# Three of the last output stores, cut into unequal runs of partitions

## The chip, the core and the metric

The kernel runs on one core of a Trainium2 chip. A core has five engines that work side by side: TensorE (matrix products, PE in the profile), VectorE (DVE), ScalarE (ACT), GpSimd (POOL) and SyncE (SP), which here issues the transfers. The transfers between the chip's large memory (HBM) and the core's working memory (SBUF, 128 partitions) are carried out by 16 DMA engines. The metric is the device time of one execution in microseconds (us), the median of several runs; lower is better.

## The reference

The computation has two stages. The first is an attention through 49 "agent" vectors per batch: the agents attend to all keys of a batch and gather a value each, and then each query attends to the 49 agents.

```
a2k = softmax(scale * agents @ k^T);  agent_v = a2k @ v        # per batch, 49 x 128
q2a = softmax(scale * q @ agents^T);  x = q2a @ agent_v        # 12,544 x 128 per batch
```

The second is a feed-forward block on all 4 x 12,544 = 50,176 rows, with a maximum over three products:

```
h = max(max(x @ w1, x @ w2), x @ w3);  out = h @ w_out         # 128 -> 768 -> 128
```

q, k, v and the output have 50,176 x 128 numbers of 4 bytes each, 25.7 MB apiece, so the kernel moves more than 100 MB through the DMA engines.

## The kernel before

The keys and values of a batch are loaded in pieces of up to four groups of seven tiles (a tile is 128 rows), cast to 16 bits, turned, scored against the agents and summed up. When a batch's 49 agent values are known, the feed-forward weights are folded into small tables for that batch (`G`), so that a query row needs only its 49 attention weights and these tables. A count made on the chip (`fullest`) decides between this short way and a general way (`in_general`); with the inputs here the short way is taken.

The queries are worked in 49 groups `s` of eight tiles (1,024 rows); 48 of them lie within a batch, and group 48 (`NQ - 1`) gathers the last two tiles of each of the four batches. Three groups share one load of q (`q_load`) and one output buffer of 128 partitions x 24 tile rows (`OS`, five of them). For each group the program casts q (POOL), turns it (PE), copies it out (ACT), scores it (PE), takes exponentials (ACT), makes the sums and two hidden products (PE), takes their maximum (ACT and DVE), makes the output product (PE) and scales it into the output buffer, in two halves of four tiles (`out_scale`; steps `ov.s.0` and `ov.s.1`).

A partition of the output buffer holds consecutive output rows, so a store is 128 pieces, one for each partition. Up to group 44, three groups are stored by one transfer (12 KB from each partition, 1,536 KB in all). Groups 45 and 46 are stored alone (step `st.45`, `st.46`: 4 KB from each partition, 512 KB), group 47 in two halves (`st.47.0`, `st.47.1`: 2 KB from each partition, 256 KB), and group 48 alone, with 1 KB pieces, 512 KB.

The order of the work is written out by hand in `ORDER`; each engine does its own steps in that order, and waits on semaphores where a step needs another engine's result. All stores and loads of this stage are issued by SyncE, one after another, from the function `store` (line 497) and its counterparts for loads (lines 288, 332, 489). At the end of `ORDER` stand

```
... st.44 x.45/1 ex.47/0 x.46/2 p.45/7,5 su.47 p.46/1,2 ov.45.0/1 u.47/0
re.47/3 v.47/4 ov.45.1 a.47/0 ov.46.0 st.45 ov.46.1 x.47/0 st.46 p.47/3,7 ov.47.1 ov.47.0 st.47.0 st.47.1
```

so group 48 is stored before group 44's buffer, and the last four transfers of the program are `st.45`, `st.46`, `st.47.0` and `st.47.1`. No later step uses their buffers again; the program's end (line 753 in the profile) waits until all stores have landed. Line 209 loads the agents, a transfer of 49 partitions issued by ScalarE at the start.

Of the kernel before, what the change touches and what calls it, by code (L numbers as in the profile page):

```python
# [16 lines left out]
P, H, C, A, B, NT, GT, KT, NF = 128, 64, 128, 49, 4, 98, 8, 7, 6  # L17
# [7 lines left out]
CAPACITY = 64  # L25
TG, TK = 3, 4
LONG = TG * GT

PE, ACT, DVE, POOL, SP = range(5)

SLOTS = {"M": 8, "LD": 5, "QB": 3, "KB": 3, "VB": 4, "KT": 3, "QT": 3, "EQ": 8, "EK": 4, "AS": 3, "R": 3, "RC": 9, "OS": 5}
SHAPE = {"LD": ([P, max(TK * KT, LONG), C], FP32), "QB": ([P, GT, C], BF16), "KB": ([P, KT, C], BF16), "VB": ([P, KT, C], BF16),
         "KT": ([P, KT * C], BF16), "QT": ([P, GT, P], BF16), "EQ": ([P, 512], BF16), "EK": ([P, KT * A], BF16),
         "AS": ([P, 512], BF16), "R": ([P, 512], BF16), "RC": ([P, GT], FP32), "OS": ([P, LONG, C], FP32)}

# [158 lines left out]
class Emit:  # L194
# [277 lines left out]
    def far(self, name, s, n):  # L472
# [6 lines left out]
        row = (z // WHOLE * NT + z % WHOLE * GT) * P  # L479
        rows = flat[row:row + LONG * P, :].rearrange("(p j) c -> p j c", j=LONG)  # L480
        return rows if n == LONG else rows[:, s % TG * GT:(s % TG + 1) * GT, :]

    def near(self, s, tile_, n):
        if s == NQ - 1:
            return tile_[:, :GT, :].rearrange("p (b j) c -> p b j c", j=2)
        return tile_[:, :LONG, :] if n == LONG else tile_[:, s % TG * GT:(s % TG + 1) * GT, :]

    def q_load(self, s):
        return lambda: self.nc.sync.dma_start(self.near(s, self.t[f"q.{s}"], LONG), self.far("q", s, LONG))

    def store(self, s, h=None):
        def fn():
            n = LONG if s < NQ - 1 - TG else GT
            far, near = self.far("out", s, n), self.near(s, self.t[f"os.{s // TG * TG}"], n)
            if h is not None:
                far, near = (x[:, self.tiles(s, h), :] for x in (far, near))
            self.nc.sync.dma_start(far, near)
        return fn

    def tiles(self, s, h, mixed=False):  # L500
# [257 lines left out]
```

## Time and profile before

| what | value |
|---|---|
| time, median of 3 runs | 257.96 us (257.70 to 258.14) |
| span of the profiled execution, first to last instruction | 256.1 us |
| busy: PE, DVE, ACT, POOL | 187.4, 163.3, 145.3, 145.7 us |
| DMA: moved in the span, mean rate | 105.00 MB, 410 GB/s |
| HBM read and written | 78.74 and 25.69 MB |

The profile has no other time of the profiled execution than its span; the runs' median is 1.9 us more, which is what lies around the first and the last instruction.

The page's second part cuts the span into 40 equal slices of 6.4 us, one digit or number for each: a digit is a busy share in tenths. Its third part counts DMA packets by queue: q1 is the queue that SyncE fills, q10 ScalarE's, and q8 and q14 bring instructions to the engines. Its sixth part, and the list of DMA issues, name each kind of transfer by where it goes and where it comes from, with how often it was issued, its size, and the median time from issue to landing. A row of a view by stages gives a stretch of the span, its length, the busy time of each computing engine with its count of instructions, the granted clock of TensorE, the mean busy share of the 16 DMA engines and their rate. A row on a line's instructions gives the shortest, the median and the longest duration in nanoseconds, and when the first and the last of them began.

### The profile page before, as it was taken

How to read it: one execution, taken by the hardware profiler on the slowest of the kernel's cores; microseconds unless marked ns; L12 is line 12 of the kernel's file. 1: busy time of each engine (PE TensorE's matmuls, PEld its weight loads, DVE VectorE, ACT ScalarE, POOL GpSimd, SP SyncE). 2: the span in 40 equal slices, each digit the busy share in tenths (PEclk: the TensorE clock that was granted, in tenths of full speed). 3: DMA queues.
4: the chain of work that ended last, by engine and by line, in shares of the span. 5: the costliest groups of instructions: out<-in, count | busy, mean ns of one | idle time of the engine just before them, and what ended most of it. 6: DMA issues, size and time to landing. Idle time of an engine off the chain costs nothing. (4 is left out here: it accounts for less than half of the span.)

```text
span 256.1 us, 7498 instructions
## 1 busy us (share of the span) xinstructions
PE 187.4 (73%) x3070; PEld 136.6 (53%) x3105; DVE 163.3 (64%) x336; ACT 145.3 (57%) x240; POOL 145.7 (57%) x164
## 2 busy tenths in 40 slices
PE   0684675869698779895986898778687779998400
PEld 0472543757475558674774677356464465664200
DVE  4443523837677868765699954724739989888700
ACT  2445357347585657573767656546256868887300
POOL 2252752998789279787975897468364443440000
PEclk9996599799999959998899999979979999999955
DMA  7999999999999999999999999999999999999993
GB/s 252 438 418 422 420 428 425 422 425 423 421 415 424 430 424 426 428 417 426 416 431 427 419 429 420 432 424 425 420 430 424 420 421 425 425 424 425 414 360 103
DMA packets 11526, 105.00 MB, mean 410 GB/s; under 512 B 1175, under 2 KB 2395, under 8 KB 4443
## 3 DMA queue, kind: packets, MB, share of 16 engines
q1 hardware_dynamic: 11280, 104.34, 97.2%
q8 instruction: 26, 0.43, 0.7%
q10 hardware_dynamic: 203, 0.10, 0.2%
q14 instruction: 17, 0.14, 0.1%
HBM read 78.74 MB, written 25.69 MB: 408 GB/s over the span
## 5 line engine op out<-in xcount | busy, mean ns | idle before, releaser
L298 POOL CAST KB<-LD 128x896 bf16<-128x896 f32 x56 | 51.8, 964 | 38.1 <-DMA LD<-in_k_dram 36.8
L508 POOL CAST QB<-LD 128x1024 bf16<-128x1024 f32 x49 | 49.8, 1048 | 33.4 <-PE psum L271 17.3
L568 DVE TENSOR_TENSOR OS<-psum,RC 128x512 f32<-128x512 f32 x97 | 60.7, 676 | 9.1 <-DMA out_dram<-OS 5.3
L514 ACT ACTIVATE QT<-psum 128x1024 bf16<-128x1024 bf16 x49 | 50.2, 1024 | 21.3 <-PE psum L303 19.6
L309 DVE COPY KT<-psum 128x896 bf16<-128x896 bf16 x56 | 34.5, 620 | 32.6 <-PE psum L303 28.6
L303 PE MATMUL psum<-ident,KB 128*128 128x128 bf16 x392 | 37.0, 246 | 11.7 <-POOL KB L298 9.9
L527 ACT ACTIVATE EQ<-psum 128x512 bf16<-128x512 f32 x49 | 29.3, 598 | 21.9 <-PE psum L271 16.0
L298 POOL CAST VB<-LD 128x896 bf16<-128x896 f32 x42 | 38.2, 949 | 4.9 <-DMA LD<-in_v_dram 4.6
L318 ACT ACTIVATE EK<-psum 128x343 bf16<-128x343 f32 x56 | 25.3, 460 | 24.7 <-PE psum L271 15.5
L303 PEld LDWEIGHTS <-KB 128*128 128x128 bf16 x392 | 28.4, 111 | 18.9 <-POOL KB L298 15.4
L547 ACT ACTIVATE AS<-psum 128x512 bf16<-128x512 f32 x49 | 29.2, 599 | 13.5 <-PE psum L271 12.4
L550 DVE TENSOR_TENSOR R<-psum,AS 128x512 bf16<-128x512 f32 x49 | 32.5, 678 | 6.4 <-PE psum L271 3.1
L303 PE MATMUL psum<-ident,QB 128*128 128x128 bf16 x392 | 31.5, 226 | 6.4 <-POOL QB L508 5.7
L303 PEld LDWEIGHTS <-QB 128*128 128x128 bf16 x392 | 25.8, 101 | 15.6 <-POOL QB L508 8.4
L271 PE MATMUL psum<-QT,agT 128*128 128x512 bf16 (+1 forms) x82 | 25.7, 380 | 6.7 <-ACT QT L514 5.9
L271 PEld LDWEIGHTS <-EQ 49*128 49x128 bf16 (+1 forms) x588 | 20.7, 97 | 16.3 <-ACT EQ L527 7.6
L271 PE MATMUL psum<-EQ,G 128*128 128x512 bf16 (+1 forms) x91 | 28.0, 367 | 1.3 <-issue 0.6
L271 PEld LDWEIGHTS <-VB 128*128 128x128 bf16 x392 | 16.6, 97 | 17.6 <-ACT VB L296 8.7
L271 PE MATMUL psum<-EK,VB 128*128 128x49 bf16 x392 | 19.7, 187 | 6.0 <-ACT VB L296 5.0
L271 PE MATMUL psum<-G,EQ 49*128 49x128 bf16 x392 | 21.4, 225 | 0.9 <-DVE OS L568 0.5
L271 PE MATMUL psum<-agT,KT 128*128 128x49 bf16 x392 | 20.5, 191 | 1.4 <-DVE KT L309 0.9
L271 PE MATMUL psum<-G,R 64*128 64x128 bf16 x392 | 20.5, 225 | 1.4 <-DVE R L550 1.4
(83 smaller groups left out, 180.7 us busy)
## 6 DMA issues: line engine op xcount, KB each, us to landing
LD<-in_q_dram SPq DMA_DIRECT2D x16, 1536.0 KB, 17.2
out_dram<-OS SPq DMA_DIRECT2D x15, 1536.0 KB, 20.0
LD<-in_k_dram SPq DMA_DIRECT2D x12, 1792.0 KB, 16.0
LD<-in_v_dram SPq DMA_DIRECT2D x12, 1792.0 KB, 16.7
LD<-in_k_dram SPq DMA_DIRECT2D x4, 896.0 KB, 16.4
LD<-in_v_dram SPq DMA_DIRECT2D x4, 896.0 KB, 14.6
out_dram<-OS SPq DMA_DIRECT2D x3, 512.0 KB, 13.0
LD<-in_moe_w_dram SPq DMA_DIRECT2D x3, 384.0 KB, 13.4
```

The source lines that it names most:

```text
L271: self.nc.tensor.matmul(out, w, x, start=start, stop=True, skip_group_check=True)
L298: self.nc.gpsimd.tensor_copy(out=out, in_=src)
L303: self.nc.tensor.transpose(t[:, j * P:(j + 1) * P], src[:, j, :], self.ident)
L309: return lambda: self.nc.vector.tensor_copy(out=self.t[f"kT{r}"], in_=self.t[f"kT_ps{r}"].bitcast(BF16)[:, :KT * C])
L318: return lambda: self.nc.scalar.activation(self.t[f"e{r}"], self.t[f"s{r}"][:, :KT * A], AF.Exp, scale=SCALE)
L508: return lambda: self.nc.gpsimd.tensor_copy(out=self.t[f"qb.{s}"], in_=self.half("q", s))
L514: return lambda: self.nc.scalar.activation(self.t[f"qT.{s}"].rearrange("p j c -> p (j c)"), self.t[f"qT_ps.{s}"].bitcast(BF16), AF.Copy)
L527: return lambda: self.nc.scalar.activation(self.t[f"e.{s}"], self.t[f"qs.{s}"], AF.Exp, scale=SCALE)
L547: return lambda: self.nc.scalar.activation(self.t[f"a.{s}"], self.t[f"u.{s}"], AF.Relu)
L550: return lambda: self.nc.vector.tensor_tensor(out=self.t[f"r.{s}"], in0=self.t[f"v.{s}"], in1=self.t[f"a.{s}"], op=ALU.max)
L568: self.nc.vector.tensor_tensor(out=out, in0=src, in1=rc.unsqueeze(2).to_broadcast([P, 4, C]), op=ALU.mult)
```

## The change

A table `PARTS` names two stores, by group and half: the store of group 45, whole, and the first half of group 47's. `store` now issues a store as a sequence of transfers over consecutive runs of partitions: 124 and 4 for group 45, 68 and 60 for the first half of group 47, and all 128 at once (`P` is 128) for every other store, as before. The same bytes go to the same places. SyncE issues two transfers more than before, 22 stores in place of 20.

```diff
 TG, TK = 3, 4
 LONG = TG * GT
+PARTS = {(45, None): (124, 4), (47, 0): (68, 60)}
...
             far, near = self.far("out", s, n), self.near(s, self.t[f"os.{s // TG * TG}"], n)
             if h is not None:
                 far, near = (x[:, self.tiles(s, h), :] for x in (far, near))
-            self.nc.sync.dma_start(far, near)
+            first = 0
+            for rows in PARTS.get((s, h), (P,)):
+                self.nc.sync.dma_start(far[first:first + rows], near[first:first + rows])
+                first += rows
         return fn
```

## The prediction

> **What bounds the kernel now.** I read the page's slices first, then SyncE's waits, then the busy time by stage at the end, then the DMA queues and issues. The page:
>
> ```profile
> span 256.1 us, 7498 instructions
> DMA  7999999999999999999999999999999999999993
> GB/s 252 438 418 422 420 428 425 422 425 423 421 415 424 430 424 426 428 417 426 416 431 427 419 429 420 432 424 425 420 430 424 420 421 425 425 424 425 414 360 103
> ```
>
> All 16 DMA engines are busy from the second slice to the last but two, at about 425 GB/s, so the kernel is bound by bytes moved. The last slices (6.4 us each) fall to 360 and 103 GB/s: the drain is not level. The waits of SyncE's queue over the last 20 us say who waits for that drain:
>
> ```profile
> SPq L753 <- DMA out_dram<-OS: 11.2, 2, 10.6
> SPq L497 <- DVE OS L568: 4.3, 3, 2.1
> ```
>
> L753 is the end of the program. SyncE stands there 10.6 us in one wait, for stores to land. The last store (the second half of group 47) has these rows among the store line's instructions:
>
> ```profile
> L497 SPq DMA_DIRECT2D out_dram<-OS x1: 615/615/615, 242.6 to 242.6; - x1
> DMA to landing us min/median/max: 11.9/11.9/11.9
> ```
>
> Issued at 242.6 and landed 11.9 us later, at 254.5 (254.6 unrounded). From there to the span's end lie 1.5 us of closing semaphores. So the end is set by the engine that empties its queue last. The stages (length; then busy time of PE, PEld, DVE, ACT, POOL; granted clock, DMA share, GB/s):
>
> ```profile
> 240.00:242.00 2.00, 0.40 (x8) 0.23 (x8) 1.51 (x3) 0.53 (x3) 0.00 (x0) 1.00 0.99 415
> 245.00:246.00 1.00, 0.00 (x0) 0.00 (x0) 0.00 (x0) 0.00 (x0) 0.00 (x0) 0.50 1.05 371
> 246.00:247.00 1.00, 0.00 (x0) 0.00 (x0) 0.00 (x0) 0.00 (x0) 0.00 (x0) 0.50 0.78 326
> 247.00:248.00 1.00, 0.00 (x0) 0.00 (x0) 0.00 (x0) 0.00 (x0) 0.00 (x0) 0.50 0.80 328
> 248.00:249.00 1.00, 0.00 (x0) 0.00 (x0) 0.00 (x0) 0.00 (x0) 0.00 (x0) 0.50 0.77 317
> 249.00:250.00 1.00, 0.00 (x0) 0.00 (x0) 0.00 (x0) 0.00 (x0) 0.00 (x0) 0.50 0.69 281
> 251.00:252.00 1.00, 0.00 (x0) 0.00 (x0) 0.00 (x0) 0.00 (x0) 0.00 (x0) 0.50 0.52 141
> 252.00:253.00 1.00, 0.00 (x0) 0.00 (x0) 0.00 (x0) 0.00 (x0) 0.00 (x0) 0.50 0.29 88
> 253.00:254.00 1.00, 0.00 (x0) 0.00 (x0) 0.00 (x0) 0.00 (x0) 0.00 (x0) 0.50 0.16 61
> 254.00:255.00 1.00, 0.00 (x0) 0.00 (x0) 0.00 (x0) 0.00 (x0) 0.00 (x0) 0.50 0.01 4
> ```
>
> Share times 16 is the number of engines still at work. From 246 to 249 it is about 12.5: some four engines are through by about 247. A fifth goes at about 249.5 (share 0.69, 11). At 251 to 252 eight work, at 252 to 253 four or five, at 253 to 254 two or three, and nothing much after 254.1. Between the first engine and the last lie some 7 us; a level drain would end earlier.
>
> How a store is spread over the engines is read from the packet counts of the whole span:
>
> ```profile
> DMA packets 11526, 105.00 MB, mean 410 GB/s; under 512 B 1175, under 2 KB 2395, under 8 KB 4443
> q1 hardware_dynamic: 11280, 104.34, 97.2%
> q8 instruction: 26, 0.43, 0.7%
> q10 hardware_dynamic: 203, 0.10, 0.2%
> q14 instruction: 17, 0.14, 0.1%
> LD<-in_q_dram SPq DMA_DIRECT2D x16, 1536.0 KB, 17.2
> out_dram<-OS SPq DMA_DIRECT2D x15, 1536.0 KB, 20.0
> LD<-in_k_dram SPq DMA_DIRECT2D x12, 1792.0 KB, 16.0
> LD<-in_v_dram SPq DMA_DIRECT2D x12, 1792.0 KB, 16.7
> LD<-in_k_dram SPq DMA_DIRECT2D x4, 896.0 KB, 16.4
> LD<-in_v_dram SPq DMA_DIRECT2D x4, 896.0 KB, 14.6
> out_dram<-OS SPq DMA_DIRECT2D x3, 512.0 KB, 13.0
> LD<-in_moe_w_dram SPq DMA_DIRECT2D x3, 384.0 KB, 13.4
> LD<-in_q_dram SPq DMA_DIRECT2D x1, 512.0 KB, 21.6
> out_dram<-OS SPq DMA_DIRECT2D x2, 256.0 KB, 11.9
> LD<-in_moe_w_out_dram SPq DMA_DIRECT2D x1, 384.0 KB, 13.7
> ag_st<-in_agents_dram ACTq DMA_DIRECT2D x1, 98.0 KB
> ```
>
> SyncE issues 73 transfers, all of 128 partitions; ScalarE one, the agents: 49 partitions of 4 rows, 196 packets. Its queue q10 shows 203, so 7 are over. And 73 x 16 + 7 = 1175, the count under 512 B. So a transfer ends with one small packet for each engine that took part: 16 engines for 128 partitions, 7 for 49. Sixteen and seven are the largest divisors of 128 and 49 not above 16; even shares of whole partitions give just that.
>
> **The change part by part.** By that rule 124 = 4 x 31 and 4 = 4 x 1 go over four engines, 68 = 4 x 17 over four, 60 = 15 x 4 over fifteen. The Trainium skill, DMA: Bandwidth & Descriptors, section "Why a DMA increments its semaphore by 16 and not by 1", states the same rule and adds that a SyncE or ScalarE transfer takes the lowest-numbered k engines; the trace's 203 agrees with the count, and no row here shows the numbers.
>
> Bytes on each of the four engines, taking the same four each time. Store of group 45 (512 KB, 4 KB a partition): 8 partitions each before, 32 after, so 24 x 4,096 = 98,304 bytes more. First half of 47 (256 KB, 2 KB a partition): 8 before, 17 + 4 after, 13 x 2,048 = 26,624 more. On each other engine: 8 x 4,096 + 4 x 2,048 = 40,960 bytes less (one engine of them 8 x 2,048 still less, as 60 goes over fifteen).
>
> Rate of one engine: 415 / (16 x 0.99) = 26.2 GB/s in 240 to 242, and 328 / (16 x 0.80) = 25.6 in 247 to 248. So the four get 98,304 / 26.2 + 26,624 / 25.6 = 3.75 + 1.04 = 4.8 us more, the others 1.6 us less. No other work hides it: after 242.6 only stores run, and the end waits for the last engine of all.
>
> The rest is small. SyncE issues two transfers more, by the store line's and the agents' rows:
>
> ```profile
> L497 SPq DMA_DIRECT2D out_dram<-OS x20: 332/346/2782, 67.7 to 242.6; - x20
> L209 ACTq DMA_DIRECT2D ag_st<-in_agents_dram x1: 577/577/577, 0.7 to 0.7; - x1
> ```
>
> An issue costs 0.35 us, 0.58 for the one that was split unevenly, 2.8 us at worst, where the queue seems to have been full. Behind the second issue of group 45 stands the store of 46, 1.2 us later (240.4 against 239.2), which covers it; behind that of 47's first half stands its second half, pushed by 0.35 to 0.6 us. It is covered by what the engines still have queued: even the first engines work until 246.5, some four us after that issue. If the queue is full for 2.8 us per issue, the last half starts at 248, still before the late engines are through. I take nothing. No compute waits: the output buffer's places are not taken again after group 45.
>
> So the time hangs on which four engines these are. An engine that ended at f ends at f + 4.8. Against the old last end, 254.1, it is harmless only for f below 249.3, and by the stages only four engines, or a fifth just about, are that early. Lower bound: the four are the early ones; they end at 247.5 + 4.8 = 252.3, the others at 254.1 - 1.6 = 252.5, which is 1.6 us gained. Upper bound: one of the four is the last engine, 4.8 us lost.
>
> Which of them is nearer? All wide transfers are shared evenly, so what makes an engine late is work beside them: instruction fetches (26 of 16 KB, 0.7% of 16 x 256.1 us, 1.1 us each, and 17 smaller ones) and the agents' load on its seven. Joining packet records end to start, I find only one of the early engines among the seven that took the agents. No view prints that, so it chooses between the cases and sets no term. If a split by four takes four of those seven, at least three late engines get the extra bytes. The latest of three out of eleven late ones ends, by the stages, between 253 and 254.1; I take 253.7. Sum: 253.7 + 4.8 - 254.1 = 4.4 us more, span 260.5. The profiled execution is told by its span alone, 256.1; the median of the runs is 257.96, 1.9 us above it for what lies around. Forecast: 257.96 + 4.4 = 262.4.
>
> **The rivals.** (1) Faster: the four engines are the early ones. Price -1.6 us, 256.4. It decides from the point where all four are through by about 249. For it: four engines are early, and the amount moved would just level the drain (252.3 against 252.5). Against it: the joined packets.
>
> (2) Nothing moves: the split is over all engines whatever the rows, or the pace is set by where a partition is read and not by the engine that reads it. Then a row moved to an idle engine still waits behind the rows of its old neighbours, the drain ends where it ended, and two issues of 0.35 us are covered: 258.0. Against the first half: 203 packets. For the second: all stages run at one rate near 425 GB/s, whatever the transfer. The Trainium skill, the same page, section "Where 436 GB/s comes from", holds that the SBUF's 16 ports of 27.2 GB/s are what limits; the 26.2 above is near it, and no row parts engine from port. By it, rival 1 would gain nearly nothing, and the forecast would come out somewhat worse, since rows read through one port by two engines go slower.
>
> (3) Slower, but less: the three others of the four are the earliest of the late ones, through by 251.4: 251.4 + 4.8 - 254.1 = 2.1 us, 260.1. (4) Slower still: the last engine is among them and shares ports at half pace for the last 1.5 us: 4.8 + 1.5 = 6.3, 264.3.
>
> **How the numbers follow.** Forecast 0.55, rival 1 0.24, rival 2 0.08, rival 3 0.09, rival 4 0.04. About 0.2% is what a measurement can tell (0.5 us). Faster 0.24, same 0.08, slower 0.68. The likeliest case alone reaches from 260.1 to 263.6 (4.8 plus 0.8 for shared ports). Leaving rival 1 out would leave more than 2 in 10 outside, so the range goes down to it: 256.2 to 263.6.
>
> **What the changed profile would show.** The count under 512 B: 1175 before; two more issues on 4 + 4 + 4 + 15 engines in place of 16 + 16 make it 1170. If it is 1207, all 16 were used. The stages: after 253 a share of about 0.2 (three or four engines) for some 5 us, with the last landing near 259 and SyncE's wait at L753 near 15 us. If the early engines took the bytes, the share stays near 1 until 251 and falls at once by 252.6. My forecast fails at its one weak step, which engines the split by four takes; the sizes before it come from counts.

## The result and the profile after

The changed kernel takes 261.14 us (median of 4 runs, 260.94 to 261.93) against 257.88 us for the kernel before on the same chip. The ratio is 1.0129, with a 95% interval of 1.0115 to 1.0144: 3.3 us slower. The forecast was 262.4, 4.4 us slower than the 257.96 it started from. Two stores are cut, those of group 45 and of the first half of group 47, though the title speaks of three.

The page of the changed kernel, in 40 slices of now 6.5 us, and its packet counts:

```profile
span 259.3 us, 7500 instructions
DMA  7999999999999999999999999999999999999961
GB/s 254 438 413 426 423 425 425 419 423 428 420 418 426 427 426 427 420 430 419 417 433 425 426 421 428 426 415 425 429 423 428 417 434 421 427 422 421 391 239 41
DMA packets 11521, 105.00 MB, mean 405 GB/s; under 512 B 1170, under 2 KB 2390, under 8 KB 4438
```

Up to the last three slices nothing has changed; there the rate is 391, 239 and 41 GB/s, against 414, 360 and 103 before. The count of small packets is the forecast 1170: the two cut stores went over 4 + 4 + 4 + 15 engines, not over 16 each.

SyncE's waits over the end, and the last store among the store line's instructions (line 500 now, which was 497):

```profile
SPq L757 <- DMA out_dram<-OS: 11.8, 4, 9.6
L500 SPq DMA_DIRECT2D out_dram<-OS x1: 1357/1357/1357, 244.6 to 244.6; - x1
DMA to landing us min/median/max: 13.3/13.3/13.3
```

The last store is issued at 244.6 (242.6 before) and lands 13.3 us later, at 257.9 (254.6 before). The forecast had SyncE's wait at the program's end near 15 us. It is 11.8 us in four pieces, the longest of 9.6, against 11.2 in two before, the longest of 10.6, because SyncE came to it 2.7 us later: the last issue began 2 us later and took 1.4 us in place of 0.6, as if the queue were full, though no view shows how full it is. So the wait does not tell the loss; the landing does, 3.3 us. The end by stages (length, then busy time of PE, PEld, DVE, ACT, POOL, granted clock, DMA share, GB/s):

```profile
249.00:250.00 1.00, 0.00 (x0) 0.00 (x0) 0.00 (x0) 0.00 (x0) 0.00 (x0) 0.50 0.81 315
250.00:251.00 1.00, 0.00 (x0) 0.00 (x0) 0.00 (x0) 0.00 (x0) 0.00 (x0) 0.50 0.48 180
251.00:252.00 1.00, 0.00 (x0) 0.00 (x0) 0.00 (x0) 0.00 (x0) 0.00 (x0) 0.50 0.39 117
252.00:253.00 1.00, 0.00 (x0) 0.00 (x0) 0.00 (x0) 0.00 (x0) 0.00 (x0) 0.50 0.22 76
253.00:254.00 1.00, 0.00 (x0) 0.00 (x0) 0.00 (x0) 0.00 (x0) 0.00 (x0) 0.50 0.26 100
254.00:255.00 1.00, 0.00 (x0) 0.00 (x0) 0.00 (x0) 0.00 (x0) 0.00 (x0) 0.50 0.15 59
255.00:256.00 1.00, 0.00 (x0) 0.00 (x0) 0.00 (x0) 0.00 (x0) 0.00 (x0) 0.50 0.13 51
256.00:257.00 1.00, 0.00 (x0) 0.00 (x0) 0.00 (x0) 0.00 (x0) 0.00 (x0) 0.50 0.06 25
257.00:258.00 1.00, 0.00 (x0) 0.00 (x0) 0.00 (x0) 0.00 (x0) 0.00 (x0) 0.50 0.04 14
```

Share times 16 again: from 252 to 254 about four engines work (0.22, 0.26), then two (0.15, 0.13), then one. The twelve others are through by about 252, some two microseconds sooner than before. The time went to a few engines that drain alone.

### The profile page after: what moved, and what is told of

It is laid out like the page before. It is cut to its first block, busy times and chain, and to the rows that moved or that the text cites. A ratio compares the mean times of both kernels' runs of the same rounds, so it can differ in the third digit from the quotient of the medians.

```text
span 259.3 us, 7500 instructions
## 1 busy us (share of the span) xinstructions
PE 188.9 (73%) x3070; PEld 138.1 (53%) x3105; DVE 163.8 (63%) x336; ACT 145.4 (56%) x240; POOL 145.7 (56%) x164
## 2 busy tenths in 40 slices
DMA packets 11521, 105.00 MB, mean 405 GB/s; under 512 B 1170, under 2 KB 2390, under 8 KB 4438
## 4 chain that ended last, share of the span: by engine, by line
DMA 49%; PE 18%; DVE 10%; POOL 8%; ACT 5%; issue 3%; SPq 0%; DVEq 0%; ACTq 0%; POOLq 0%
DMA LD<-in_v_dram 18%; DMA LD<-in_k_dram 14%; PE psum L272 13%; DMA out_dram<-OS 9%; DMA LD<-in_moe_w_dram 5%; PE psum L304 5%; POOL VB L299 4%; DVE OS L572 3%; POOL KB L299 2%; DMA ag_st<-in_agents_dram 2%; ACT VB L297 1%; ACT EQ L531 1%; ACT QT L518 1%; POOL QB L512 1%; DVE gap L407 1%
## 5 line engine op out<-in xcount | busy, mean ns | idle before, releaser
L304 PE MATMUL psum<-ident,QB 128*128 128x128 bf16 x392 | 32.4, 229 | 6.7 <-POOL QB L512 5.9
L551 ACT ACTIVATE AS<-psum 128x512 bf16<-128x512 f32 x49 | 29.2, 600 | 11.8 <-PE psum L272 10.7
L304 PEld LDWEIGHTS <-QB 128*128 128x128 bf16 x392 | 26.5, 103 | 16.3 <-POOL QB L512 8.8
L272 PE MATMUL psum<-G,EQ 49*128 49x128 bf16 x392 | 20.8, 222 | 0.7 <-DVE OS L572 0.3
## 6 DMA issues: line engine op xcount, KB each, us to landing
LD<-in_v_dram SPq DMA_DIRECT2D x4, 896.0 KB, 14.5
```

Of the source, the lines that this page charges most:

```text
L272: self.nc.tensor.matmul(out, w, x, start=start, stop=True, skip_group_check=True)
L304: self.nc.tensor.transpose(t[:, j * P:(j + 1) * P], src[:, j, :], self.ident)
L551: return lambda: self.nc.scalar.activation(self.t[f"a.{s}"], self.t[f"u.{s}"], AF.Relu)
```

## Experiments

Each experiment changes only the table `PARTS` of the changed kernel. The times before were 257.85 us for the first four runs, 257.96 for the next four and 257.79 for the last two.

**One cut alone.**

```diff
-PARTS = {(45, None): (124, 4), (47, 0): (68, 60)}
+PARTS = {(45, None): (124, 4)}
```

> Only the store of group 45 is cut, 124 and 4. In the changed kernel the last landing came at 257.9 against 254.6 before; the two cuts together put 4.8 us on each of four engines, so the latest of the four would have landed at 253.1 without them. Theory (the four lowest engines carry the extra bytes, and the time is that of the last engine): 253.1 + 3.75 = 256.9, 2.3 us more than before, 260.2. Rival (the time follows from the number of transfers or from the queue being full when they are issued): half of the whole loss, 259.5, or nothing, as the later half store is not cut.

Measured: 260.66 us, ratio 1.0119 (1.0103 to 1.0135), 2.8 us slower; last landing 257.2.

```diff
-PARTS = {(45, None): (124, 4), (47, 0): (68, 60)}
+PARTS = {(47, 0): (68, 60)}
```

> Only the first half of group 47 is cut, 68 and 60. Theory: the four engines get 1.04 us more and the others 0.3 us less, and the four are not the last ones (253.1 against 254.6 at the landing): 253.1 + 1.04 = 254.1 against 254.6 - 0.3 = 254.3, so no loss and perhaps 0.3 us gained, 257.6 to 257.9. Rival (cost by transfer, or each cut has its own price that adds up): the loss of both less that of group 45, about 1 us, 258.9.

Measured: 258.47 us, ratio 1.0023 (1.0013 to 1.0033), 0.6 us slower; last landing 255.2. Most of the loss is group 45's, as its bytes say. The loss of 0.6 us lies between the theory's none and the rival's 1 us. The two losses add up to 3.4 against the 3.3 of both together; a maximum over engines need not have added up so neatly. The trace's semaphore updates (one for each engine of a transfer, when its share has landed) put the loss on one of the four: the part of 68 partitions lands last at 254.3 and the last store 0.9 us later, just as in the changed kernel (257.0 and 257.9). These two runs leave it open whether the latest of the four engines was a little ahead of the last one, or was itself the last and a byte cost less than the rate says.

**As many transfers, evenly cut.**

```diff
-PARTS = {(45, None): (124, 4), (47, 0): (68, 60)}
+PARTS = {(45, None): (64, 64), (47, 0): (64, 64)}
```

> Both stores cut, but 64 and 64, which 16 divides: two transfers more, as in the changed kernel, and every engine's bytes as before. Theory: no change, 257.9 (within 0.5 us); packets under 512 B 1175 + 32 = 1207. Rival (cost by transfer, or SyncE held up by a full queue): as the changed kernel, 261.1.

Measured: 257.32 us, ratio 0.9982 (0.9973 to 0.9991). Packet counts, and the last store's issue and landing:

```profile
DMA packets 11558, 105.00 MB, mean 411 GB/s; under 512 B 1207, under 2 KB 2427, under 8 KB 4475
L500 SPq DMA_DIRECT2D out_dram<-OS x1: 1102/1102/1102, 244.6 to 244.6; - x1
DMA to landing us min/median/max: 9.6/9.6/9.6
```

The last store is issued at 244.6, with SyncE held up for 1.1 us, just as in the changed kernel, and it lands at 254.2, not at 257.9. So neither the two more transfers nor the later issue is what costs: with the same number of each, the time is even 0.5 us under the kernel before. The small gain was not expected.

**The lowest engine alone.**

```diff
-PARTS = {(45, None): (124, 4), (47, 0): (68, 60)}
+PARTS = {(45, None): (96, 31, 1)}
```

> Only group 45, cut 96, 31 and 1: 96 goes over sixteen engines (6 partitions each), 31 and 1 have no divisor but 1 and should go to a single engine, the lowest. That engine gets 30 partitions of 4 KB more, 122,880 bytes, 4.7 us; the fifteen others two partitions less, 0.3 us. Theory (the lowest engine is the one early engine among the four): it ends at 247.5 + 4.7 = 252.2, the last at 0.3 us less than before: 257.6, not slower. Rival (the lowest engine is as late as the others, or one engine alone cannot keep its pace): 251.5 to 254 + 4.7, 1.5 to 4.7 us more, 259.5 to 262.6.

Measured: 257.26 us, ratio 0.9975 (0.9966 to 0.9984). Packet counts, the last store's landing and the end by stages:

```profile
DMA packets 11528, 105.00 MB, mean 411 GB/s; under 512 B 1177, under 2 KB 2397, under 8 KB 4445
DMA to landing us min/median/max: 9.6/9.6/9.6
252.00:253.00 1.00, 0.00 (x0) 0.00 (x0) 0.00 (x0) 0.00 (x0) 0.00 (x0) 0.50 0.25 86
253.00:254.00 1.00, 0.00 (x0) 0.00 (x0) 0.00 (x0) 0.00 (x0) 0.00 (x0) 0.50 0.02 8
```

1175 and two more is 1177: the parts of 31 and of 1 partition each ended with one small packet, so each went over one engine. That engine bore 4.7 us more, nearly what each of the four bears in the changed kernel, and the drain ended no later: it was one of the early ones. The Trainium skill, DMA: Bandwidth & Descriptors, section "Why a DMA increments its semaphore by 16 and not by 1", has a split by one, two or four begin at the same lowest engine. The runs agree so far as the one engine that is early here is also among the four (below); the number of an engine stands in no view.

**The bytes of one more store.**

```diff
-PARTS = {(45, None): (124, 4), (47, 0): (68, 60)}
+PARTS = {(45, None): (124, 4), (46, None): (124, 4), (47, 0): (68, 60)}
```

> The changed kernel, with the store of group 46 cut 124 and 4 as well: the four engines get another 98,304 bytes each, 3.75 us by the rate of the profile. This tells two readings of the size apart. Reading A (a byte costs an engine what the profile's rate says, and the latest of the four would have ended about 1 us ahead of the last engine): the last landing moves by the full 3.75, from 257.9 to 261.7, time 261.1 + 3.75 = 264.9. Reading B (the latest of the four was the last engine of all, and the bytes moved cost 0.7 of the price, as 3.3 against 4.8, 2.8 against 3.75 and 0.6 against 1.04 suggest): 0.7 x 3.75 = 2.6, time 263.7.

Measured: 265.02 us, ratio 1.0269 (1.0255 to 1.0284). That is 3.9 us over the changed kernel, for the 3.75 of reading A and the 2.6 of reading B: A holds. The end by stages:

```profile
252.00:253.00 1.00, 0.00 (x0) 0.00 (x0) 0.00 (x0) 0.00 (x0) 0.00 (x0) 0.50 0.27 109
253.00:254.00 1.00, 0.00 (x0) 0.00 (x0) 0.00 (x0) 0.00 (x0) 0.00 (x0) 0.50 0.28 117
254.00:256.00 2.00, 0.00 (x0) 0.00 (x0) 0.00 (x0) 0.00 (x0) 0.00 (x0) 0.50 0.26 103
256.00:258.00 2.00, 0.00 (x0) 0.00 (x0) 0.00 (x0) 0.00 (x0) 0.00 (x0) 0.50 0.20 81
258.00:260.00 2.00, 0.00 (x0) 0.00 (x0) 0.00 (x0) 0.00 (x0) 0.00 (x0) 0.50 0.13 50
260.00:262.00 2.00, 0.00 (x0) 0.00 (x0) 0.00 (x0) 0.00 (x0) 0.00 (x0) 0.50 0.06 25
```

Here the four engines stand by themselves: a share of a quarter from 252 to 256, four of sixteen, and then three, two and one. Each runs at about 25 GB/s (103 / (16 x 0.26)), near the 26.2 with all sixteen at work. The trace's semaphore updates for the part of 124 partitions come at 249.1, 250.9, 253.1 and 254.9: the four are not alike, the first is 5.8 us ahead of the fourth. SyncE was held up more here: three of its issues took 2.3 to 3.4 us, and the last store was issued only at 249.4. That cost nothing, for twelve engines had landed their share of it by 252.7, and the other four did at 256.6 to 262.2.

**The two lowest engines.**

```diff
-PARTS = {(45, None): (124, 4), (47, 0): (68, 60)}
+PARTS = {(45, None): (80, 46, 2)}
```

> Only group 45, cut 80, 46 and 2: 80 goes over sixteen engines (5 each), 46 and 2 over two (23 + 1 each), so the two lowest engines get 21 partitions of 4 KB more, 3.3 us, the others 0.5 us less. The lowest engine was seen to bear 4.7 us. Theory (of the four only the lowest is early): the second ends past the old end, if it would have ended after 251.3 (254.6 - 3.3): up to 3 us more, 258.5 to 261. Rival (the two lowest are both early, and the loss comes from the third and fourth): 0.3 to 0.5 us less, 257.4.

Measured: 257.99 us, ratio 1.0004 (0.9995 to 1.0013): no change. Each of the two got 3.3 us more and neither made the end later, so the second is through early as well, if less so; the rival's gain did not come either. Together with the four landings above: two of the four have time to spare, the third and the fourth have not, and the loss comes from these. The changed kernel's own trace agrees: the part of 68 partitions lands on the four at 253.4, 253.7, 255.5 and 257.0, and the last four updates of the last store come 0.9 to 1.0 us behind these, at 254.3, 254.6, 256.4 and 257.9. Two lie no later than the old end, 254.6, and two behind it.

**Even cuts: what they do by themselves.**

```diff
-PARTS = {(45, None): (124, 4), (47, 0): (68, 60)}
+PARTS = {(45, None): (96, 32)}
```

> Only group 45, cut 96 and 32, both over sixteen engines: no byte changes its engine's total, one transfer more. The 96, 31 and 1 cut gained 0.6 us and the 64 and 64 cuts gained 0.5 us. If the gain of 96, 31 and 1 is the lowest engine's help (0.3 us by the bytes), this one gains nothing: 257.85. If a cut as such gains (a transfer more, other partitions for each engine), it gains as the others did: 257.3.

Measured: 257.59 us, ratio 0.9984 (0.9975 to 0.9993). A cut that moves no byte between engines gains 0.4 us, most of what the cut 96, 31 and 1 gained. So the run with 96, 31 and 1 shows that the lowest engine can bear 4.7 us at no cost; a gain from its help is not shown.

```diff
-PARTS = {(45, None): (124, 4), (47, 0): (68, 60)}
+PARTS = {(45, None): (96, 31, 1), (47, 0): (64, 64)}
```

> Group 45 cut 96, 31 and 1 (the lowest engine helps), the first half of 47 cut 64 and 64. If the two gains are separate things they add: 257.85 - 0.6 - 0.5 = 256.8. If both are the same thing (a later issue of the last stores, or the cut as such), 257.3 again.

Measured: 257.64 us, ratio 0.9987 (0.9975 to 0.9999). The gains do not add; if anything there is less than with either cut alone.

```diff
-PARTS = {(45, None): (124, 4), (47, 0): (68, 60)}
+PARTS = {(44, None): (64, 64), (45, None): (64, 64), (46, None): (64, 64), (47, 0): (64, 64), (47, 1): (64, 64)}
```

> The stores of groups 42 to 44, 45, 46 and both halves of 47 are cut 64 and 64: five transfers more, no engine's bytes changed. If each cut over sixteen engines gains by itself (one gained 0.4 us, two 0.5 us), five gain more, 256.9 or less. If the gain is a single small shift of when the last stores are issued, it stays at 0.3 to 0.6 us, 257.4. If a full queue holds SyncE up, the last store comes late: 258.5 or more.

Measured: 260.63 us, ratio 1.0110 (1.0091 to 1.0129), 2.8 us slower with the same bytes on every engine. The page counts 1255 small packets, 1175 and 5 x 16: every part went over sixteen engines. The store line's last issues and their landings, and then the stages:

```profile
L500 SPq DMA_DIRECT2D out_dram<-OS x2: 588/978/1367, 251.4 to 252.8; - x2
DMA to landing us min/median/max: 3.2/3.6/4.0
```

```profile
250.00:252.00 2.00, 0.00 (x0) 0.00 (x0) 0.00 (x0) 0.00 (x0) 0.00 (x0) 0.50 0.61 201
252.00:254.00 2.00, 0.00 (x0) 0.00 (x0) 0.00 (x0) 0.00 (x0) 0.00 (x0) 0.50 0.63 174
254.00:256.00 2.00, 0.00 (x0) 0.00 (x0) 0.00 (x0) 0.00 (x0) 0.00 (x0) 0.50 0.36 88
```

The last two stores are issued at 251.4 and 252.8, nine and ten microseconds after the last computing instruction, and land within 3.2 to 4.0 us: now it is the issue that is late. SyncE's issues took up to 2.8 us each, which I read as a full queue, and from 252 to 254 ten engines still work (0.63 x 16) where four or five, and then two or three, did before. So two more transfers were covered in the changed kernel, but five are not.

**The same cut far from the end.**

```diff
-PARTS = {(45, None): (124, 4), (47, 0): (68, 60)}
+PARTS = {(2, None): (124, 4)}
```

> No store of the end is cut; the first store of the run (groups 0 to 2, 12 KB from each partition, issued near 68 us) is cut 124 and 4. Each of the four engines gets 24 x 12,288 = 294,912 bytes more, 11.3 us by the rate of the profile. Theory (an engine that falls behind while all are fed evenly never catches up): the latest of the four, about 1.1 us ahead of the last engine without it, ends the run: 11.3 - 1.1 = 10.2 us more, 268.1. Rival (behind lies time enough to make up for it; only a cut at the end costs): 258 to 260.

Measured: 273.21 us, ratio 1.0601 (1.0583 to 1.0618), 15.4 us slower. The page's slices (of 6.8 us) and the longest of SyncE's waits between 80 and 115 us:

```profile
DMA  7999999999999974899999999999999999999960
GB/s 265 436 419 414 429 422 427 423 420 425 426 422 415 420 292 176 316 413 418 335 431 381 424 425 402 432 424 419 430 427 427 420 426 408 420 429 417 393 242 18
SPq L289 <- DMA LD<-in_q_dram: 17.8, 1, 17.8
```

Three stages, in the middle and at the end:

```profile
100.00:102.00 2.00, 0.00 (x0) 0.00 (x0) 0.00 (x0) 0.00 (x0) 0.00 (x0) 0.50 0.26 111
104.00:106.00 2.00, 0.83 (x7) 0.48 (x5) 0.17 (x1) 1.02 (x1) 1.80 (x3) 0.50 0.26 113
267.00:269.00 2.00, 0.00 (x0) 0.00 (x0) 0.00 (x0) 0.00 (x0) 0.00 (x0) 0.50 0.07 29
```

The cost is not made up over the 190 us that follow; it is half as large again as the forecast 10.2 us. SyncE waits 17.8 us in one piece for a load of q, and the slices fall to 292, 176 and 316 GB/s: a load is there when its slowest engine is through, so everything waits for the four engines in the middle of the run. The semaphore updates show it: that load, issued at 72.0, lands on twelve engines by 84.3 and on the four at 97.0, 98.3, 99.8 and 102.3, and from 100 to 106 four engines work alone (a share of 0.23 to 0.26). Before, the same load had landed on all at 87.8. So 14.5 of the 15.4 us stand there already, 34 us after the cut store was issued. The forecast priced the bytes at 26.2 GB/s, 11.3 us; the fourth engine was later than that, and why was not taken apart. At the end one engine alone is still behind (0.07 x 16 is one).

## Why the prediction was right, and where its size was off

**The split.** "124 = 4 x 31 and 4 = 4 x 1 go over four engines, 68 over four, 60 over fifteen" is right: 1170 small packets, 1177 with 31 and 1, 1207 with 64 and 64.

**The price.** 98,304 bytes more on an engine were to cost 3.75 us. One store more cost 3.9 us, once the four engines alone set the end. The rival in which the place of reading sets the pace would have shown no loss there, and falls. Half pace beside the other engines (rival 4) was not seen either: in that same run the four early engines had landed group 44's store between 243.2 and 243.9, and the first of the four, taken to be the lowest engine, landed its 31 partitions of group 45, 126,976 bytes, at 249.1, while between fourteen and seven engines were at work in all (shares of 0.88 to 0.42 from 243 to 249). That is 5.2 to 5.9 us, 21.5 to 24.5 GB/s, less than 26.2 but far from half. The Trainium skill's ceiling of the ports (DMA: Bandwidth & Descriptors, section "Where 436 GB/s comes from") bore on these stores by that little at most, as far as this run shows. No run shows the 0.8 us for shared ports in the upper end of the range.

**Which engines.** This was the weak step, and it held in its sign. Rival 1, the early engines, fell: four, then two, then one engine drain alone for six microseconds in the changed kernel. Yet "at least three late engines get the extra bytes" was one too many: two ended behind the old end. The lowest engine is early, as the argument had it, and the second has time enough as well. The sign needed only one late engine among the four. The prediction had chosen by joined packet records, which no view prints, and gave this case little more than even odds (0.55).

**The size.** The term that was mis-sized is the end of the latest of them: "between 253 and 254.1; I take 253.7". The landing moved 3.3 us where 4.8 us of bytes were added, so in the same measure the latest ended at 254.1 + 3.3 - 4.8 = 252.6. Group 45's cut alone gives 254.1 + 2.6 - 3.75 = 253.0, and the run with one store more 254.1 + 7.6 - 8.5 = 253.2. With 253 in place of 253.7 the sum would have been 3.7, against 3.3 measured. What is left is of the size by which this end moves between programs: the cut of 47 alone gives 254.1 + 0.6 - 1.0 = 253.7.

The traces suggest a reason, which no run tested. Before, these were the issues of the stores of 45 and 46 and their landings:

```profile
L497 SPq DMA_DIRECT2D out_dram<-OS x1: 332/332/332, 239.2 to 239.2; - x1
DMA to landing us min/median/max: 12.0/12.0/12.0
L497 SPq DMA_DIRECT2D out_dram<-OS x1: 333/333/333, 240.4 to 240.4; - x1
DMA to landing us min/median/max: 13.0/13.0/13.0
```

They landed at 251.2 and 253.4. Group 46's store is 32,768 bytes on each engine, 1.25 us at 26.2 GB/s; the last landing came 2.2 us later. So about 1 us of the old end was a stop of the late engines and not their bytes. In that stretch instruction fetches ran (one packet of 16 KB took 1.0 us from 250.5 on, three of 8 KB began between 250.7 and 251.7), and single 4 KB packets of the stores took up to 1.19 us where most took 0.16. In the changed kernel the fourth engine had no such stop: it landed its small part of group 45 at 254.5 and its share of 46 at 255.7. Taking 4.85 us for its 31 partitions from their landing at 254.3 puts it at 249.4 for group 44's store, which landed on the last engine at 250.1: some 0.6 us ahead. By this reading the 0.4 us that the prediction put between the two was not far off; what was missed is that the old end held a stop of 1 us that the fourth engine was spared. The two make 1.6 us, for the 1.5 between 252.6 and 254.1.

**What was costed at nothing.** The longer issues were covered, as said: 64 and 64 had as late an issue and no loss. The cover is thin: five transfers more and it is gone.

**The rivals of no change and of a smaller loss.** No change is out. Rival 3 (2.1 us) and the forecast (4.4 us) bracket the 3.3 us.

**A slip that changed nothing.** The one engine that the 60 partitions leave out got 8 x 2,048 bytes less from that store in place of 4 x 2,048, so 8,192 less than the others and not "8 x 2,048 still less".

## What to carry to other kernels

In these runs the number of partitions of a transfer decided how many DMA engines carried it: take a number that 16 divides, because 124 partitions were carried by four engines, and these moved 31 each in place of 8. In this kernel, which moves bytes all the time, the engines did not make that up: cut at the first store, 190 us before the end, the loads waited for the slowest of the four, and the whole delay reached the end. An uneven split can be used to lean on an early engine, but only once it is shown which engines are early, for instance by giving one of them work and looking whether the end moves.

## What had not been expected

A cut into two parts that each go over all sixteen engines gained 0.4 to 0.5 us (ratios 0.9984 and 0.9982), twice with intervals clear of 1, while five such cuts lost 2.8 us. The loss is told by the late issue. The gain was not tested, but the traces show where it lies: in the four runs that gained (the two even cuts and the two with 96, 31 and 1) group 46's store landed 1.1 to 1.4 us after group 45's, without the stop of the late engines, against 2.2 us before and 1.8 us in the runs with 68 and 60 alone and with 80, 46 and 2, which gained nothing. What spares them the stop is not shown. The fastest kernel of the study, 96, 31 and 1, is 0.25% under the kernel before (0.9966 to 0.9984); its interval overlaps those of the even cuts, so nothing beyond their gain is shown.
